# Turning q', k' and the normalised x with VectorE blocks and DMAs in chunks 3 to 5 of a gated linear attention with MLP

## The chip, the cores and the metric

The kernel runs on one core of a Trainium2 chip. Its engines work in parallel, each through its own list of instructions in order: TensorE (PE, with its weight loads as PEld), VectorE (DVE), ScalarE (ACT), GpSimd (POOL) and SyncE (SP), which here issues nearly all transfers; the transfers themselves run on 16 DMA engines. The metric is the device time of one execution in microseconds, lower is better.

## The reference

```python
# gla_recurrent: q, k, v, alpha are (B=4, H=8, S=768, D=48)
for t in range(S):
    state = alpha[:, :, t, :, None] * state + np.einsum('bhd,bhe->bhde', k[:, :, t], v[:, :, t])
    y[:, :, t] = np.einsum('bhd,bhde->bhe', q[:, :, t], state)
# bridge: (B, H, S, D) -> (B, S, H*D = 384)
x = np.ascontiguousarray(y.transpose(0, 2, 1, 3)).reshape(B, S, H * D)
# metaformer_identity: w_ch1 is (384, 1536), w_ch2 is (1536, 384)
mu = np.mean(x, axis=-1, keepdims=True)
var = np.mean((x - mu) ** 2, axis=-1, keepdims=True)
xn = (x - mu) / np.sqrt(var + 1e-06) * g_ln
out = x + np.maximum(xn @ w_ch1, 0.0) @ w_ch2
```

All is float32; the weights come as float64 and are rounded on the chip.

## The kernel before

The sequence is cut into 6 chunks of 128 steps; with 4 batch entries that makes 24 attention turns `attention(c, b)`. In the order they have the letters a to x: chunk c and batch entry b have letter number 4c + b, so m to p are chunk 3, q to t chunk 4 and u to x chunk 5. A "batch" below is one such turn.

One attention turn works as follows. ScalarE takes the logarithm of alpha (`la`, L292); TensorE sums it along the steps with a triangular matrix (`lps`, L303); ScalarE makes of the sum the decay `eq` and its inverse (L306, L307). VectorE makes k' = k times the inverse decay (L309) and q' = q times the decay (L311), side by side in a tile `qk` with the 128 steps on the partitions. The decay at the end of each half chunk goes to DRAM as `row` (L316) and comes back as the column `gate` (L378).

For the scores, q' and k' are needed with the head's 48 elements on the partitions and the steps along the row. TensorE turns them: for each of the two, four transpositions of 128x112 into one PSUM tile `tps` (L336), which ScalarE (in chunk 0 for k' VectorE) copies to the SBUF tiles qT and kT (L343, L341). These are the operands of the scores `aps` (L360). VectorE masks the scores into `at` (L372). TensorE makes the state updates `ups` from k' and v (L388); VectorE and GpSimd put them through the gate into the states (L401, L403). The output `yps` adds scores times v and qT times state (L426, L429).

The output goes to a DRAM tile `kept` (L452, to be read back as `ob` for the residual, L493), is normalised by ScalarE to `xn` (L460 to L470), and TensorE turns it with three transpositions of 128x128 into `xps` (L476). From there VectorE (chunks 0 and 1) or ScalarE (chunks 2 to 5, three instructions, L483) writes it to the chunk's tile xT, multiplied by g_ln. xT holds all four batch entries of a chunk, and the MLP starts when it is complete.

The MLP of chunk 0 is plain: `hps` (L506) and `ops` (L518). Chunks 1 to 5 use a scheme with fewer products of blocks: sums of blocks of xT are made first (`combine_x`, L769, letter X), then 30 hidden products (L795) whose results VectorE and GpSimd add up; ScalarE applies the ReLU (L846, letter R); sums of hidden blocks are made (`combine_hidden`, L605, letter N); 20 projections (L618) are added to `ob`, and finished quarters are sent (`send`, L497).

Who does what when is written out by hand: each letter of the string `ORDER` resumes one of these generators until its next `yield`. M is the MLP of the chunks 1 to 5, V the hidden products of chunk 5, A to L the rounding of the weights, S and W sums of weights, Y, Z, P, Q the MLP of chunk 0, O the loads of `ob`. Since each engine works in order, `ORDER` fixes the list of every engine, the queue of SP among them: a transfer that waits for its data holds up all transfers behind it. All transfers of the kernel but two small ones at the start are issued on SP.

Tiles come from pools with a fixed number of buffers per tag; a new tile waits until the oldest buffer's readers are done. qT and kT share the tag `sum` (11 buffers) with the sums of blocks and the partial results `u`; the input tiles ra, rk, rq have the tag `in` (6 buffers), with two batch entries in each tile. From chunk 3 on `load_one` loads alpha, k and q of one batch, two batches ahead; it is called right after the step at L316.

Of the kernel before, what the change touches and what calls it, by code (L numbers as in the profile page):

```python
# [9 lines left out]
FP32 = mybir.dt.float32  # L10
# [5 lines left out]

EPS = 1e-6
STAGED = 3

# [1 line left out]


ORDER = (
    "acacababcdaacabdbaabdcacabbacbbababceccbaAcfcdbadaacecacfeafdeeeabfddaddbbbceeeA"
    "caecdfeedcgadeehbbbbeegfgbgdhddgaAbaghffffgbdgAgehefhffgecfffBddccicdChjfcYehhhc"
    "fhfcdieYdgggehghejhgjfhffdfYhjjjjidBZYBZeiZijZijAhghgiBghiiijBZCZZkCCYkiZiijlYij"
    "lejjkYhgYkiZDYhZZhkDYYZggYkkkljkhfhgDCkiEilEYlgEFEYDlZZFlZhgliFYFjillYYYYZjHHlmk"
    "lSklkjlGkYkYYGZZZZiZZZlnGiinmZHgmgglllmkmngYIQimYmjmmInjmQjlGikoIkmOIfheHlkkSjjo"  # L30
    "hkghhiSiJnJmmmmmkSPoPknnJoPeLjSPKkQSeeenLjKnnQpOKnepOSnOlonSffpfnLmnWnmmSSPPSfmP"
    "pghPfjhmmgpSXlmjXXkXXkXkinkQSXWXmnSQOXQQlXiMkiiiXWMWnMMMMSlMMMSSMMkpMMMMMMMoMMnr"
    "oMMoMoWpkqpopMMMMOnqopoopoprmRRmpWpopnMpRpmMoqqnMWrqMMqWRRMMMMMMMWMpMMMMMMMOMqqq"
    "lMMpMMjMjMMMqMpMMqnrrsjoRRRrostMtRqoqqqqoppnooWqpqWoNWNMqRRRMMNNqMMNNsMsslONNsNM"
    "MMMMMMMMMMMMNpmmNMWNmMMqllpllooONMoMMMMMpNNttoMMtosumssMMNrMMrrrMMstMMMrXXXXXXXs"
    "vqqqrvrrXXXMMMMMXrrMMMMMMMMMMMMMMnMnRpJnOqopOMMMMMMMMMMMMMMMMMMMMMMMMpMpRMMtMMRM"
    "MOnMRttrnrurMssssttttsrrvvvrsrstttRtRMtMMtMRuuMtMRRNRtMRuNNNMMMMMRNNMNMMMruqNMMM"
    "MMMMooMMMsssNNNqMqNvNvMvwvMxMMMMNMMMMvNNuuuusrsvuwsquuuuvuuuMussxxvsxvvtvtXvXXww"
    "wXXwXXXXMMMMMMMMMMMMMMMMMXXxMMMMMMMMMMMMMMMMMMMMsvvOORtxtstRttOrMMMMMMMMMMMMMMMM"
    "MMMMMMMxRxMMtxxwrwwwrMMMsxMRwxRwxwxxwwvRxxwuwRvqwRRRuuMwMNMMMMrOxRMRMNMstMxMwNNN"  # L40
    "NNMxxxwwwwwxxNMNMuuNxMwwMNuuNMMMMMxMuMMMNMMMMqNrwXNNXvvvXvvMMuMMXXXXXOMMMMMMMMXM"
    "MOMMMMXXMMMMMMMMMMMMMMMMMMMMMMMMMMMMMMMMMMMMMMMMMRMMMMMMMMMMRRRRMMMMMRuRRROOxMMw"
    "RvNMNNNxRNRvNNNNMMMMMMMMMMMMMNNNXXXXXXXXXXXMMMMMMNVVMMMMVVVVVVVVVVVVVVMMNNVVKVVV"
    "VVVVVVVVOVVVVVVVVMMVVVVVVVVVVVVVVVVVVVVNVVVRRRRRRRRRRRRMMMMMNNNNNONLMMMMONMMNNNN"
    "MMMMMMMMMMMNNMOMMMMMMMMMMMMMNNMMMMMMNMMMMMMMMM"
)


# [1 line left out]
def kernel(  # L50
# [60 lines left out]
    HS = P // 2  # L111
    halves = [slice(HS * s, HS * s + HS) for s in range(2)]
    r = np.arange(P)
# [5 lines left out]
    def load_exchanged(t, src):  # L119

        for h in range(2):
            nc.sync.dma_start(t[halves[h]].rearrange("t i p d -> t (i p d)"),
                              src[halves[1 - h]].rearrange("t h d -> t (h d)"))

    def load(c, m, names):

        bs = range(2 * m, 2 * m + 2)
        rows = slice(c * P, (c + 1) * P)
        for n, src in (("a", alpha), ("k", k), ("q", q)):
            if n in names:  # L130
# [9 lines left out]
                raws.update({(n, c, b): t[:, b - bs.start] for b in bs})  # L140
        if "v" in names:
# [19 lines left out]
    def load_one(n):  # L161

        c, b = divmod(n, B)
        for n, src in (("a", alpha), ("k", k), ("q", q)):
            if n not in lone:
                lone[n] = raw.tile([P, 2, 2, NP, D], FP32, name=f"r{n}", tag="in", bufs=6)
            t = raws[n, c, b] = lone[n][:, b % 2]
            rows = src[b, c * P:(c + 1) * P]
            if n == "a" and b % 2:
                load_exchanged(t, rows)  # L170
                continue
            nc.sync.dma_start(t.rearrange("t i p d -> t (i p d)"),
                              rows.rearrange("t h d -> t (h d)"))
# [92 lines left out]
    def qk_of(c, b):  # L266
        return qks[b if c < 2 else b % 3]
# [10 lines left out]
    def attention(c, b):  # L278
# [39 lines left out]
        n = c * B + b + 2  # L318
        if c < 2 and b % 2:
            load(c + 1, b // 2, "akq")  # L320
        elif n == 3 * B + 1:
            load_one(n - 1)
            load_one(n)
        elif 3 * B + 1 < n < NCB * B:
            load_one(n)
        yield
# [4 lines left out]
        kT = work.tile([R, NP, 2, HS], FP32, name="kT", tag="sum", bufs=11)  # L331
        qT = work.tile([R, NP, 2, HS], FP32, name="qT", tag="sum", bufs=11)
        for i in range(2):
            tps = ps.tile([R, NP, P], FP32, name="tps", tag="bank", bufs=8)
            for p in range(NP):
                nc.tensor.transpose(  # L336
                    tps[:, p], qk_of(c, b)[:, i, p].rearrange("p a b -> p (a b)")[:, :R], ident)
            yield
            tv = tps.rearrange("r p (s t) -> r p s t", s=2)
            if i:  # L340
                (nc.vector.tensor_copy if whole else nc.scalar.copy)(out=kT, in_=tv)  # L341
            else:
                nc.scalar.copy(out=qT, in_=tv)  # L343
            yield
# [84 lines left out]
                            nc.tensor.matmul(yps[r][halves[s], i, p], of, by, start=True, stop=True)  # L429
        yield  # L430
        x = work.tile([P, DM], FP32, name="x", tag="row", bufs=8)
        few = work.tile([P, 5], FP32, name="few", tag="few", bufs=8)
        mean, dev, rstd, off, more_of = (few[:, i:i + 1] for i in range(5))
        act = nc.scalar.activation
        yps = [y.rearrange("t a b d -> t (a b d)") for y in yps]
# [35 lines left out]
        yield  # L471
        if c not in xT_of:
            xT_of[c] = work.tile([P, NF, B, P], FP32, name="xT", tag="xT")
        xps = ps.tile([P, NF, P], FP32, name="xps", tag="bank", bufs=8)
        for f in range(NF):
            nc.tensor.transpose(xps[:, f], xn[:, f * P:(f + 1) * P], ident)  # L476
# [112 lines left out]
    def combine_hidden(c):  # L589
        a, ready = blocks_of(c)  # L590
        n0, n2, n6, n9, n5, n13 = (
            work.tile([P, NT, P], FP32, name=f"sum{i}", tag="sum", bufs=11) for i in range(6))
# [17 lines left out]

    def product(c, n):
        if n == SECOND[0]:
            u = [work.tile([P, 512], FP32, name="u", tag="sum", bufs=11) for i in range(3)]
# [135 lines left out]
    def combine_x(c):  # L749
# [3 lines left out]
            buffers_of_last()  # L753
            new = late_of["x"]
        for i in range(0 if new else 5):
            t = work.tile([P, NT, P], FP32, name=f"sum{i}", tag="sum", bufs=11)
# [20 lines left out]
    def hidden_product(c, r, n):  # L777
# [4 lines left out]
        if n == FIRST[0]:  # L782
            for i in range(3):
                u = late_of["u"][i] if c + 1 == NCB else work.tile(
                    [P, 512], FP32, name="u", tag="sum", bufs=11)
# [123 lines left out]
```

## Time and profile before

| | |
|---|---|
| three runs | 431.96, 433.00, 433.22 us; median 433.0 |
| profiled execution | 433.49 us, of which the profile's span covers 431.6 |
| turns of q' and k', L336 | 192, in the span from 10.1 to 286.3 us; chunks 3 to 5 have half of them |
| turns of x, L476 | 72, from 29.3 to 351.5 us; chunks 3 to 5 have half |
| copies of qT and kT by ScalarE | 44 in all, 586 and 593 ns each |
| scaling of xT by ScalarE, L483 | 48, 365 ns each |
| to landing, median | `kept` 2.8 us, `ob` 2.5, `gate` 4.6, v 6.0 |
| SP's longest sums of waits | for results to send (L497) 60.7 us on GpSimd and 41.4 and 33.0 on VectorE; for the decay (L316) 40.4 on ScalarE |

A share of busy time is a mean over the span. TensorE's instructions overlap, so the length of one (274 ns for a transposition) is more than the distance from one to the next; the distance is read from the chain of waits, where a run of equal instructions stands with its count and length. TensorE's granted clock is full throughout.

### The profile page before, as it was taken

Reading aid. Unit: us, or ns where it says so; the run is one execution under the profiler, and the core shown is the slowest. Engines: PE = TensorE matmul, PEld = TensorE weight load, DVE = VectorE, ACT = ScalarE, POOL = GpSimd, SP = SyncE. Lnnn points to the kernel's source line nnn. Section 1 sums busy time; section 2 is a strip of 40 time slices with the busy share of each in tenths; the row PEclk is TensorE's granted clock in tenths of the full one; section 3 lists DMA queues with packets and bytes.
Section 4 is the critical chain, followed back from the end, with each engine's and each line's share of the span. In section 5 each row is a group of like instructions: output and inputs, shape, how many; then the busy total and the mean of one; then the engine's idle time right before and its main releaser. Section 6 shows DMA issues by size and latency. Waiting matters only on the chain.

```text
span 431.6 us, 11685 instructions
## 1 busy us (share of the span) xinstructions
PE 423.8 (98%) x4760; PEld 378.5 (88%) x4760; DVE 333.0 (77%) x644; ACT 202.4 (47%) x519; POOL 153.1 (35%) x164
## 2 busy tenths in 40 slices
PE   7999998999999999999999999999999999999997
PEld 5889887876678989998899999899998899989996
DVE  3897889789989879958569876567686669856972
ACT  5587654567454754462664351654821461125100
POOL 1012020020113665052674223771044660468414
PEclk9999999999999999999999999999999999999999
DMA  8968878498017343343006033300122000101021
GB/s 252 283 181 259 260 218 288 105 292 256 5 58 220 79 128 94 94 148 93 0 4 175 10 79 115 69 3 2 56 75 91 2 1 2 36 2 37 27 65 55
DMA packets 55517, 45.53 MB, mean 106 GB/s; under 512 B 26748, under 2 KB 51580, under 8 KB 55464
## 3 DMA queue, kind: packets, MB, share of 16 engines
q1 hardware_dynamic: 54920, 44.63, 35.5%
q8 instruction: 37, 0.61, 0.6%
q10 hardware_dynamic: 544, 0.17, 0.2%
q14 instruction: 16, 0.13, 0.1%
HBM read 35.25 MB, written 9.53 MB: 104 GB/s over the span
## 4 chain that ended last, share of the span: by engine, by line
PE 96%; DMA 1%; SPq 0%; issue 0%; DVE 0%; ACT 0%; DVEq 0%
PE ops L618 30%; PE hps L795 30%; PE hps L506 7%; PE ops L518 7%; PE tps L336 5%; PE aps L360 4%; PE ups L388 3%; PE yps L426 2%; PE yps L429 2%; PE xps L476 2%; DMA rq<-in_q_dram 1%; PE lps L303 1%; PE aps L352 1%; PE yps L414 1%; SPq L137 0%
## 5 line engine op out<-in xcount | busy, mean ns | idle before, releaser
L634 POOL TENSOR_TENSOR ob<-ob,u 128x192 f32<-128x192 f32 x40 | 28.2, 714 | 82.9 <-DVE ob L631 61.8
L795 PE MATMUL hps<-sum,w 128*128 128x256 f32 x192 | 47.4, 380 | 0.0
L403 POOL TENSOR_TENSOR mid<-mid,gate 112x192 f32<-112x192 f32 x20 | 13.6, 681 | 78.8 <-DVE mid L401 35.7
L618 PE MATMUL ops<-w,hT 128*128 128x192 f32 x224 | 40.2, 327 | 0.0
L795 PEld LDWEIGHTS hps<-sum,w 128*128 128x128 f32 x192 | 35.9, 190 | 4.6
L618 PEld LDWEIGHTS ops<-w,hT 128*128 128x128 f32 x224 | 36.7, 190 | 0.3
L795 PE MATMUL hps<-xT,w 128*128 128x256 f32 x136 | 34.5, 380 | 0.0
L846 ACT ACTIVATE hT<-hT 128x512 f32<-128x512 f32 x48 | 27.6, 628 | 13.6 <-DVE hT L838 4.5
L506 PE MATMUL hps<-xT,w 128*128 128x256 f32 x144 | 33.2, 383 | 0.0
L518 PE MATMUL ops<-w,hT 128*128 128x384 f32 x96 | 32.6, 489 | 0.0
L506 PEld LDWEIGHTS hps<-xT,w 128*128 128x128 f32 x144 | 26.6, 190 | 3.6 <-issue 0.2
L618 PE MATMUL ops<-ws,sum 128*128 128x192 f32 x160 | 28.8, 326 | 0.0
L628 DVE TENSOR_TENSOR ob<-ops,ob 128x192 f32<-128x192 f32 x50 | 17.1, 352 | 14.8 <-PE ops L618 4.5
L795 PEld LDWEIGHTS hps<-xT,w 128*128 128x128 f32 x136 | 25.5, 190 | 3.3
L460 ACT ACTIVATE xn<-x,few 128x384 f32<-128x384 f32 x24 | 14.7, 615 | 27.8 <-DVE few L456 27.4
L518 PEld LDWEIGHTS ops<-w,hT 128*128 128x128 f32 x96 | 17.7, 190 | 10.8
L618 PEld LDWEIGHTS ops<-ws,sum 128*128 128x128 f32 x160 | 26.3, 190 | 0.1
L814 POOL TENSOR_TENSOR hT<-hT,u 128x512 f32<-128x512 f32 x8 | 10.2, 1276 | 41.5 <-DVE u L813 41.5
L336 PE MATMUL tps<-consts,qk 128*112 128x128 f32 x176 | 23.5, 274 | 1.2 <-DVE qk L311 1.2
L336 PEld LDWEIGHTS tps<-consts,qk 128*112 128x112 f32 x176 | 20.0, 134 | 4.1 <-DVE qk L311 1.8
L618 PE MATMUL ops<-ws,hT 128*128 128x192 f32 x128 | 23.4, 326 | 0.0
L343 ACT COPY qT<-tps 112x512 f32<-112x512 f32 x24 | 14.1, 586 | 18.6 <-PE tps L336 18.4
(243 smaller groups left out, 1178.9 us busy)
## 6 DMA issues: line engine op xcount, KB each, us to landing
ws<-in_moe_w_ch_dram SPq DMA_DIRECT2D x12, 768.0 KB
vn<-in_v_dram SPq DMA_DIRECT2D x12, 384.0 KB, 6.0
kept<-x SPq DMA_DIRECT2D x24, 192.0 KB, 2.8
ob<-kept SPq DMA_DIRECT2D x24, 192.0 KB, 2.5
out_dram<-ob SPq DMA_DIRECT2D x19, 192.0 KB, 1.9
ra<-in_alpha_dram SPq DMA_DIRECT2D x14, 192.0 KB, 4.9
rk<-in_k_dram SPq DMA_DIRECT2D x6, 384.0 KB
rq<-in_q_dram SPq DMA_DIRECT2D x6, 384.0 KB, 4.9
```

Source lines behind the costliest of these rows:

```text
L336: nc.tensor.transpose(tps[:, p], qk_of(c, b)[:, i, p].rearrange("p a b -> p (a b)")[:, :R], ident)
L343: nc.scalar.copy(out=qT, in_=tv)
L360: nc.tensor.matmul(aps[0][halves[i if cross else 1 - i], p, s], kT[rs, p, s], qT[rs, p, s], start=True, stop=True)
L403: nc.gpsimd.tensor_mul(new, new, by)
L460: act(out=xn, in_=x, func=AFT.Square, bias=mean, accum_out=dev)
L506: nc.tensor.matmul(hps, w1[:, j // 2, f, j % 2 * P:][:, :P], xT_of[0][:, f, bs], start=(f == 0), stop=(f == NF - 1))
L518: nc.tensor.matmul(ops_of[b], hT_of[c][:, j, b], w2[:, j], start=(j == 0), stop=(j == NJ - 1))
L618: nc.tensor.matmul(acc, lhs[:, j], rhs[:, j], start=(j == 0), stop=(j == NT - 1))
L628: nc.vector.tensor_add(x, acc, x)
L634: getattr(nc.gpsimd, f"tensor_{op}")(x, x, y)
L795: nc.tensor.matmul(acc[:, i], w, b, start=True, stop=True)
L846: nc.scalar.activation(out=x, in_=x, func=AFT.Relu)
```

## The change

For the batches m to x (chunks 3 to 5, `turned`: letter number 12 and up) TensorE's turns are replaced:

- q and k of a batch are loaded into one joined tile `rj`, side by side (`load_joined`), in place of two tiles.
- After q' and k' are made, one VectorE instruction transposes each 32x32 block of the 128x768 elements of both, back into the joined tile.
- `turn_out` moves the blocks to their places: four DMAs write 32 partitions each to a DRAM tile `rows`, in pieces of 32 elements (128 bytes).
- Only then does `load_one` of the batch after next follow, since it writes to the same joined tile.
- Four DMAs read qT and kT from `rows`, in runs of 128 elements (512 bytes). The copies from PSUM are dropped.
- xn is turned in the same way: a VectorE block transposition (128x384) into a new tile `xt`, four DMAs to `xrows`, one DMA back into xT, and three ScalarE multiplications by g_ln in place.

The tag `sum` has 12 buffers in place of 11, the tag `few` 5 in place of 8. `ORDER` is a new string throughout, from the first lines on; it has 1578 letters in place of 1566.

```diff
+TURNED = 12
...
+    def turned(c, b):
+        return c * B + b >= TURNED
+
+    def load_joined(c, b, t):
+
+        for i, (n, src) in enumerate((("q", q), ("k", k))):
+            raws[n, c, b] = t[:, i]
+            nc.sync.dma_start(t[:, i].rearrange("t i p d -> t (i p d)"),
+                              src[b, c * P:(c + 1) * P].rearrange("t h d -> t (h d)"))
+        raws["j", c, b] = t.rearrange("t n i p d -> t (n i p d)")
+
+    def turn_out(rows, t):
+
+        for a in range(4):
+            nc.sync.dma_start(rows.rearrange("(k j) t -> j k t", j=32)[:, :, 32 * a:32 * (a + 1)],
+                              t[32 * a:32 * (a + 1)].rearrange("j (k i) -> j k i", i=32))
...
+        if not turned(c, b):
+            qT, kT = turned_tiles()
+        if turned(c, b):
+            joined = raws.pop(("j", c, b))
+            nc.vector.transpose(
+                out=joined, in_=qk_of(c, b).rearrange("t n p i c -> t i n p c")[:, :, :, :, :D])
+            yield
+            rows = dram.tile([2 * DM, P], FP32, name="rows", tag="rows")
+            turn_out(rows, joined)
+            yield
+            load_next()
+            yield
+            qT, kT = turned_tiles()
+            src = rows.rearrange("(i n p d) t -> i n d p t", i=2, n=2, p=NP)
+            for i, t in enumerate((qT, kT)):
+                for h in range(2):
+                    nc.sync.dma_start(t[64 * h:64 * h + D].rearrange("r p s t -> r p (s t)"),
+                                      src[h, i])
+            yield
+        for i in range(0 if turned(c, b) else 2):
             tps = ps.tile([R, NP, P], FP32, name="tps", tag="bank", bufs=8)
...
-        few = work.tile([P, 5], FP32, name="few", tag="few", bufs=8)
+        few = work.tile([P, 5], FP32, name="few", tag="few", bufs=5)
...
+        if turned(c, b):
+            xt = work.tile([P, DM], FP32, name="xt", tag="row", bufs=8)
+            nc.vector.transpose(out=xt, in_=xn)
+            yield
+            rows = dram.tile([DM, P], FP32, name="xrows", tag="xrows")
+            turn_out(rows, xt)
+            yield
+            nc.sync.dma_start(xT_of[c][:, :, b], rows.rearrange("(f p) t -> p f t", p=P))
+            yield
+            for f in range(NF):
+                nc.scalar.mul(xT_of[c][:, f, b], xT_of[c][:, f, b], g_col[:, f:f + 1])
+            yield
+            return
         xps = ps.tile([P, NF, P], FP32, name="xps", tag="bank", bufs=8)
```

More of the change, by code (lines that the diff above doesn't have):

```diff
@@ L18 @@
 STAGED = 3
+TURNED = 12
 ORDER = (
[L26 to L43, printed above, removed]
@@ L44 @@
-    "VVVVVVVVOVVVVVVVVMMVVVVVVVVVVVVVVVVVVVVNVVVRRRRRRRRRRRRMMMMMNNNNNONLMMMMONMMNNNN"
-    "MMMMMMMMMMMNNMOMMMMMMMMMMMMMNNMMMMMMNMMMMMMMMM"
+    "acacababcdaacabdbaabdcacabbacbbababceccbaAcfcdbadaacecacfeafdbeeddddaabbcaefbeee"
+    "eafgdddafhfccghfbbefdAbbbahAdibefdbjciecejfgdfffAheeYBccffegdChhfcciedggYfdYheeh"
+    "edcicdiBggihehfYegiAgdiBidgehghghghjihhZZgZZBkjigffBfejfghjkhiiilYCiYCgCDCZYZkkZ"
+    "fZeeYgijDgYZehZhDgYYffjjjYZZkkYEYEeFggElhFjjjhihEFFijlliglZfDZZYSZZZZZYZHSfilkij"
+    "gkkjlHklZlZiIjGkSllkSlZikGlIklnYhkhkGgjGOlOYlmIjYYYYYYjmnlljjkIiHSjnekQnPeOkggJm"
@@ new lines @@
+    "hnhmkPJkgmnHkmLkJfKmnLlmfLQQQKKhSnhWWkgkPmShWonQgQXolpOljpQSkkooXolmnpmSnWmnmkXm"
+    "jnlnPmmXSoSipXnopnniOSPmppSnmommWnPPPnXiiiiipkMmSXXWnnMMXWXoXMMMSSMpMOkMWMMlMMmM"
+    "MlMMSMQWOMMkMMqMmMrMMMMRMqooorqpppppopnnlpqqpMpMMMrqOWqppqmMMMMMMMMMMjWMMMMMMoqr"
+    "MRRRMMMMMMoRrMJRMRRspRRRoMrooNMllMMMMMMMNjpWNMjMoNoRlooMNloNsrNNNqqqqqqsqqMqMMMr"
+    "MMNMrjMMrpttrjtWNsMstorrrpqqqrssrNMMMNNnnnMMXMMpptrXNMtMMMNMpMXXXXXMpptXMMsMmmmm"
+    "XMMoMMMMMXXqMMoMMMMMMMMMMMMMMtMMMMMOMnMmMMOMMMMMMMrMMMMMMMMoooMMMMMMtMpvmuRvRRRR"
@@ new lines @@
+    "RRtsrrttsvtMousssqtOtttvsssssOMMMvMvuMMusMRRRRMRomoMMMMuMuvttsMtMstNNNNNNnNNNnNN"
+    "tNNsrmrussMMvMMMMMMMnMMMxuuMMMvMMMMpMNNNrwMMMMsMMqwuuxMvvvuwvuuuuxvvtvXvLvttutXX"
+    "MMtuMMXMMXMMXusvsxXXXwMMxXxsxMMMMrxsvvMMMMMMMvvwvqqqqxMMvOXtMMwMMMMvsMMMMMuMMMMM"
+    "MMMMrMMMMMMMMMMMMMMMMMMMMMwtquRxRRRRRRRRRwwswxwxrwxxwxxxwxwORwwwMMMttMMOMMrNOwRq"
+    "NNNNNNxNNNxvqMNqxxsrMMNxrwwNwwMxrMMMMMMMMMMMMrMwMwMMNMNNMXXxXXXXXXXXOwwMMMMMMMMu"
+    "MMMMMMMMMMMMMMxxxXvMMMMMMMMMMMMMMMMMMMMMMMMMMMMMMMMMMMMMwRRRRMMOuuuuuMMMMMMMMMMM"
@@ L46 @@
+    "vwRRRRRwOxNMRMuMNOuNNRMMNMNMXuNNXXXXRXVXXXNXXVMMMMMMMMMMMMMMMMNNVVVVVVVVVVVVVVVV"
+    "VVVVVVVVVVNMNVVVVVVVVMMMNOVVVVVVVVVVVVVRRRMRRVVVNNMMRMMVVVVRRRVVRRVVORNNMMMMMMMM"
+    "MMMMNNNNNNNNNOMNONMMMMMMMMMMMMMMMMMMMMMMNNNMMMMMMMMKMMMMMM"
 )
@@ L128, in load @@
         rows = slice(c * P, (c + 1) * P)
+        joined = turned(c, bs.start)
         for n, src in (("a", alpha), ("k", k), ("q", q)):
-            if n in names:
+            if n in names and not (joined and n != "a"):
                 t = raw.tile([P, 2, 2, NP, D], FP32, name=f"r{n}", tag="in", bufs=6)
@@ L140, in load @@
                 raws.update({(n, c, b): t[:, b - bs.start] for b in bs})
+        for b in bs if joined and "k" in names else ():
+            load_joined(c, b, raw.tile([P, 2, 2, NP, D], FP32, name="rj", tag="in", bufs=6))
         if "v" in names:
@@ L163, in load_one @@
         c, b = divmod(n, B)
[L164 to L173, printed above, removed]
+        if "a" not in lone:
+            lone["a"] = raw.tile([P, 2, 2, NP, D], FP32, name="ra", tag="in", bufs=6)
+        t = raws["a", c, b] = lone["a"][:, b % 2]
+        rows = alpha[b, c * P:(c + 1) * P]
+        if b % 2:
+            load_exchanged(t, rows)
+        else:
+            nc.sync.dma_start(t.rearrange("t i p d -> t (i p d)"), rows.rearrange("t h d -> t (h d)"))
+        if b % 2 not in lone:
+            lone[b % 2] = raw.tile([P, 2, 2, NP, D], FP32, name="rj", tag="in", bufs=6)
+        load_joined(c, b, lone[b % 2])
     consts = cpool.tile([P, 2 * P + HS], FP32, name="consts")
@@ L317, in attention, with load_next @@
         yield
[L318 to L326, printed above, removed]
+        def load_next():
+            n = c * B + b + 2
+            if c < 2 and b % 2:
+                load(c + 1, b // 2, "akq")
+            elif n == 3 * B + 1:
+                load_one(n - 1)
+                load_one(n)
+            elif 3 * B + 1 < n < NCB * B:
+                load_one(n)
+        if not turned(c, b):
+            load_next()
+            yield
         at = ats[b % len(ats)]
@@ L330, in attention, with turned_tiles @@
                 "k (p s t) -> k p s t", s=2, t=HS)
-        kT = work.tile([R, NP, 2, HS], FP32, name="kT", tag="sum", bufs=11)
-        qT = work.tile([R, NP, 2, HS], FP32, name="qT", tag="sum", bufs=11)
-        for i in range(2):
+        def turned_tiles():
+            return [work.tile([R, NP, 2, HS], FP32, name=n, tag="sum", bufs=12)
+                    for n in ("qT", "kT")]
+        if not turned(c, b):
+            qT, kT = turned_tiles()
[7 more added lines that the diff above has]
+            yield
+            load_next()
+            yield
[7 more added lines that the diff above has]
+        for i in range(0 if turned(c, b) else 2):
             tps = ps.tile([R, NP, P], FP32, name="tps", tag="bank", bufs=8)
@@ L473, in attention @@
             xT_of[c] = work.tile([P, NF, B, P], FP32, name="xT", tag="xT")
+        if turned(c, b):
[9 more added lines that the diff above has]
+                nc.scalar.mul(xT_of[c][:, f, b], xT_of[c][:, f, b], g_col[:, f:f + 1])
+            yield
+            return
         xps = ps.tile([P, NF, P], FP32, name="xps", tag="bank", bufs=8)
@@ L591, in combine_hidden @@
         n0, n2, n6, n9, n5, n13 = (
-            work.tile([P, NT, P], FP32, name=f"sum{i}", tag="sum", bufs=11) for i in range(6))
+            work.tile([P, NT, P], FP32, name=f"sum{i}", tag="sum", bufs=12) for i in range(6))
         add, sub = nc.vector.tensor_add, nc.vector.tensor_sub
@@ L612, in product @@
         if n == SECOND[0]:
-            u = [work.tile([P, 512], FP32, name="u", tag="sum", bufs=11) for i in range(3)]
+            u = [work.tile([P, 512], FP32, name="u", tag="sum", bufs=12) for i in range(3)]
             win["u"] = [u[i // 2][:, i % 2 * HM:][:, :HM] for i in range(5)]
@@ L755, in combine_x @@
         for i in range(0 if new else 5):
-            t = work.tile([P, NT, P], FP32, name=f"sum{i}", tag="sum", bufs=11)
+            t = work.tile([P, NT, P], FP32, name=f"sum{i}", tag="sum", bufs=12)
             t = t.rearrange("p a t -> p (a t)")
@@ L784, in hidden_product @@
                 u = late_of["u"][i] if c + 1 == NCB else work.tile(
-                    [P, 512], FP32, name="u", tag="sum", bufs=11)
+                    [P, 512], FP32, name="u", tag="sum", bufs=12)
                 first_of["u", c, i] = u.rearrange("p (j t) -> p j t", j=2)
```

## The prediction

> **What bounds the kernel now.** I read the page first (busy shares and slices), then the chain of waits in order of time, then the groups by line and shape, last the DMA view in short windows.
>
> ```profile
> PE 423.8 (98%) x4760; PEld 378.5 (88%) x4760; DVE 333.0 (77%) x644; ACT 202.4 (47%) x519; POOL 153.1 (35%) x164
> ...
> PE   7999998999999999999999999999999999999997
> ...
> DVE  3897889789989879958569876567686669856972
> ...
> PEclk9999999999999999999999999999999999999999
> DMA  8968878498017343343006033300122000101021
> ```
> TensorE is at work in every slice at full clock; VectorE is nearly full only up to slice 13, and after a third of the span the DMA engines are mostly idle.
>
> ```profile
> 89.00 0.87 PE tps L336 x8
> 89.88 2.58 PE ops L518 x8
> ...
> 216.30 0.33 PE xps L476 x3
> ...
> 323.95 25.90 PE hps L795 x120
> 349.85 0.33 PE xps L476 x3
> 350.18 1.30 PE ops L618 x8
> ...
> 395.91 32.51 PE ops L618 x200
> 428.52 0.36 DVE ob L628
> ```
> The chain (start us, length us, what) runs along TensorE with hardly a gap, from its first transposition at 10 us to 428 us. So each turn is on the path, at its spacing in the chain and not at its 274 ns of pipelined duration: 0.87/8 = 0.109 us for one of q' and k', 0.33/3 = 0.11 us for one of x. In the same way a pass of a hidden product takes 25.90/120 = 0.216 us, of a projection 32.51/200 = 0.163 us. With these I added up TensorE's work through the list of instructions of both kernels. The old list gives 418.7 us, plus 10.5 us before the first; a step's place in the old list and its start in the trace agree within 4 us. Batches go by their letters in the order: m to p are chunk 3, q to t chunk 4, u to x chunk 5. "Place" below is that running sum in the new list, the time at which TensorE would get there without a stall.
>
> **What is removed.** Twelve turns of q' and k' (8 transpositions each) and twelve of x (3 each): 12 x (8 x 0.109 + 3 x 0.11) = 14.4 us, all on the path. ScalarE loses 24 copies of some 0.59 us (L343, L341), 14 us of an engine that is idle half the time: nothing on the path. The 36 scalings of xT stay, with SBUF in place of PSUM as source; I leave their 0.365 us.
>
> **What is added on VectorE.**
>
> ```profile
> L219 DVE SCALAR_TENSOR_TENSOR w<-ws,w 128x768 f32<-128x768 uint32 x12 | 11.7, 974 | 0.4
> L217 DVE TENSOR_SCALAR w<-ws 128x768 int32<-128x768 int32 x12 | 6.6, 552 | 0.0
> 100.00:140.00 40.00, 40.00 (x375) 28.79 (x374) 38.49 (x73) 20.20 (x57) 5.91 (x6) 1.00 0.39 119
> 140.00:280.00 140.00, 140.00 (x1636) 130.52 (x1635) 108.14 (x214) 68.83 (x180) 67.21 (x68) 1.00 0.31 84
> ```
> The first two lines are groups (busy us, mean ns), the others windows with busy us of PE, PEld, DVE, ACT, POOL. The trace has no block transposition. Passes over 128x768 take 0.55 to 0.97 us; I take 0.97, since the source is strided, and 0.55 for 128x384 (L466: 0.47, L311: 0.61). Bounds: 0.55 and 0.47 below, twice my values above, as for two passes. That is 12 x 1.52 = 18 us (12 to 36). VectorE had 32 us idle in 140 to 280 and hardly any in 100 to 140, where four large turns come. I add the durations behind the VectorE work that is placed ahead of them, and find m and n turned at about 98.6, 2 to 3 us behind their place. Cover for the rest: VectorE's idle time. If it is gone, hidden products find no free PSUM bank.
>
> **What is added on the DMA side.** Per batch 4 + 4 issues for q' and k' and 4 + 1 for x, 13 in place of none: 156 more on SP's queue (259 before), at 0.43 us (median of the stores of `kept`) 5.6 us a batch. Nobody waits for SP as such; what matters is when the data land. A store of `kept` lands 2.8 us after issue, a load of `ob` 2.5 us. Each q'k' turn writes 3072 pieces of 128 B, 192 on each of 16 engines, each x turn 96. No 128 B store is in the trace. Nearest rows, two windows of the DMA view:
>
> ```profile
> DMA packets 1012, 0.02 MB, mean 19 GB/s; under 512 B 1011, under 2 KB 1011, under 8 KB 1011
> ## 3 DMA queue, kind: packets, MB, share of 16 engines
> q1 hardware_dynamic: 1011, 0.00, 47.9%
> ...
> DMA packets 144, 0.10 MB, mean 164 GB/s; under 512 B 16, under 2 KB 144, under 8 KB 144
> ## 3 DMA queue, kind: packets, MB, share of 16 engines
> q1 hardware_dynamic: 144, 0.10, 48.4%
> ```
> From 223.9 to 225.0 only 4-byte packets of the gate run: 0.479 x 16 x 1.1 us / 1011 = 8.3 ns each. From 429.7 to 430.3 a 96 KB store of 128 rows of 768 B: 0.484 x 16 x 0.6 / 144 = 32 ns over all, 35 ns for a long one. The line between them gives 13 ns at 128 B, far nearer to the first row; I take c = 13. Bounds 8 and 35. DMA work per batch is then (192 + 96) x 13 ns = 3.7 us, and the loads back are a quarter as many pieces. With batches about 17 us apart and 31% of the engines taken, this fits.
>
> [...]
>
> **Do the data come in time?** From a large turn to the products that read qT (aps) the new list leaves 17 to 31 us of TensorE work: m, n 96 to 115; o, p 119 to 142; q 145 to 167; r 158 to 175; s, t 177 to 214; u, v 218 to 246; x 256 and w 263 to 280. One chain alone needs 1.0 (turn) + 1.7 (four issues) + 2.4 (landing) + 1.7 + 2.1 = 9 us. Three places are tight.
>
> First pair. SP's queue holds eight outward issues, six input loads (the loads into the joined buffers wait for the outward pieces, and all behind them with them), then eight loads of qT and kT. From 98.6 + 0.9: 384 pieces per engine, 0.384c; + 2.4 landing; + 9 issues, 3.9; + 2.1: 107.9 + 0.384c, against 115.4. c = 13: 112.9, in time; c = 26: 2.5 us late; c = 35: 6 us late.
>
> w. SP waits at the sends of chunk 2 until about 253.4. x's outward pieces go at 258.6; its loads wait for them, and behind those stand t's x turn, w's pieces, s's x turn, and w's loads. x's land at X = 258.9 + 0.192c (not before 260.3, the last issue) + 2.4; four loads, one of `ob` and the first of t's stores bring SP to X + 2.5; from there 0.288c for t's and w's pieces, + 2.4, + 1.7 + 2.1 for w's loads. So w lands at 275.1 for c = 13 (place 280.0), 282.5 for c = 26 and 286.8 for c = 35.
>
> u's x. Turned at 332, its four stores are out by 334.5, landed 337, read back 340, scaled (3 x 0.37) 341; combine_x of chunk 5 asks at 341, the first product of its result stands at 352. Some 5 us to spare.
>
> One moved step costs a little: the load of the input v for batches u and v (L143) now stands behind a send that waits for a projection at 240. It is issued at 242.5 and lands 6.0 us later (its median), 248.5; the update products (L388) stand at 248.1: 0.4 us. The two pool edits (`sum` 11 to 12 buffers, `few` 8 to 5) I put at nothing: at most four of `few` are alive at once in the new list, so ScalarE's later work covers it; were it gone, one more wait of a microsecond.
>
> **Sum.** Profiled execution 433.5 us (span 431.6, 1.9 around it): 433.5 - 14.4 + 0.4 = 419.5. Runs have a median of 433.0, 0.5 lower. For margins of 2.5 us at the first pair that need not hold I round up: 420.
>
> **Rivals.**
> A. Short stores cost two of my packets, c = 26: 2.5 us late at the first pair and 2.5 at w, 424.5. For: no row for 128 B stores. Against: stores of 768 and 1536 B (35 and 65 ns) lie nearly on one line with the 4-byte loads. A VectorE at twice my price (36 us) ends alike: it would be some 5 us further behind in 140 to 230, and w comes 3 us later, about 425.
> B. The other side: the DMA engines' time per piece decides, and a 128 B store costs what a 1536 B packet costs (a 192 KB store in the window 263.5 to 264.4: engines 57.9% busy over 0.9 us, 128 packets, so 65 ns). First pair 107.9 + 25.0 = 132.9, 17 us late; w, by the same steps, 21 us; o, p and r some 12 us together: 419.5 + 50 = 470. It decides from about c = 38, where first pair and w (7 and 8) eat the gain. For: four stores write into the same 512 B rows, which nothing here does now. Against: 4-byte packets take 8 ns.
> C. The queue decides, not the bytes: SP stands at a send or at a landing while a load behind it is due, 12 to 16 us over all three tight places. About 433: no change. For: SP's waits already add up to nearly 300 us, most of them at sends (L497). Against: the new list has input loads, not results, behind nearly all of these waits.
> That the turns stay on TensorE can be excluded: the new program has 132 fewer matmuls.
>
> **Chances.** Forecast 0.52 (own range 417 to 423); A 0.16; C 0.08, half of it within 0.3% (about what a measurement here can tell from no change) and the rest split to both sides; B and lesser lateness past the break-even 0.24, 0.02 of it within 0.3%. Faster 0.52 + 0.16 + 0.02 = 0.70, same 0.06, slower 0.22 + 0.02 = 0.24. The range goes from 417 (no stall, and 2 us of TensorE's old gaps gone) through A and C into the beginning of B, 437; what is left out is B's far end.
>
> **What would show it.** Right: half of the 192 turns of q' and k' and of the 72 of x gone, the chain again along TensorE with aps (L407 of the new kernel) waiting under 1 us in all for DMA; block turns near 1 us; packets of 128 B near 13 ns. Wrong: PEld waiting for a DMA of qT or kT at places 115 or 280 (A, B); DMA share near 9 tenths in 100 to 280 (B); SP in one long wait ahead of a load that TensorE then waits for (C); TensorE waiting for VectorE's sums (the VectorE variant).

## The result, and the profile after

The changed kernel takes 417.4 us (median of 4 runs, 417.42 to 419.17) against 433.0 before: ratio 0.966, 95% interval 0.963 to 0.968. Predicted were 420.0 us, 417 to 437. The profiled execution took 417.43 us, its span 415.5, where before it was 433.5 and 431.6. So 16.1 us are to be explained, and the prediction's sum has 14.0 of them.

The page after, first the busy shares and the slices, then the chain that ended last (its shares of the span by engine and by line):

```profile
PE 410.2 (99%) x4628; PEld 364.5 (88%) x4628; DVE 344.7 (83%) x668; ACT 192.7 (46%) x495; POOL 151.2 (36%) x164
...
PE   7999999999999999999999999999999999999997
...
DVE  4898899999999988997699768779767689786773
...
PEclk9999999999999999999999999999999999999999
DMA  8989987768788865336856775763314120101201
...
PE 97%; DMA 1%; SPq 1%; DVE 0%; issue 0%; DVEq 0%
```

TensorE is still the bound. It has 132 matmuls fewer, its busy time is 13.6 us shorter, and its idle time went from 7.8 to 5.3 us: 13.6 + 2.5 = 16.1. VectorE's busy time grew by 11.7 us. (The turns last 18.2 us together, but instructions that follow one another overlap: the first two turns, of 0.97 us each, take 1.83 us together.) The slices of the DMA row from the 11th on are fuller, but VectorE has 0% of the chain and the DMA engines 1%.

The waits of TensorE (us in total, times, longest). Its list has only these two:

```profile
PE tps L383 <- DVE qk L333: 1.2, 1, 1.2
PE lps L266 <- DVE more L263: 1.1, 1, 1.1
```

Both are in the first 10 us, ahead of any turned batch. Nothing in the list waits for a DMA of qT or kT.

Next the block turns (busy us, mean ns), and a window in which only pieces of 128 B run: 158 to 161 us, most of the stores of one turned batch. The DMA line gives the packets, the queue line packets, MB and the share of 16 engines:

```profile
L365 DVE STREAM_TRANSPOSE rj<-qk 128x768 f32<-128x768 f32 x12 | 11.5, 967 | 0.0
...
L523 DVE STREAM_TRANSPOSE xt<-xn 128x384 f32<-128x384 f32 x12 | 6.7, 567 | 1.0 <-ACT xn L517 1.0
```

```profile
DMA packets 2561, 0.33 MB, mean 110 GB/s; under 512 B 2560, under 2 KB 2560, under 8 KB 2560
## 3 DMA queue, kind: packets, MB, share of 16 engines
q1 hardware_dynamic: 2560, 0.32, 69.4%
```

0.694 x 16 x 3.0 us / 2560 = 13.0 ns for a piece of 128 B. The two windows that the prediction showed of before, now (busy us of PE, PEld, DVE, ACT, POOL, then clock, DMA share, GB/s):

```profile
100.00:140.00 40.00, 40.00 (x490) 28.84 (x491) 38.31 (x69) 15.24 (x45) 10.98 (x10) 1.00 0.83 204
140.00:280.00 140.00, 140.00 (x1717) 129.72 (x1713) 117.57 (x236) 69.56 (x181) 68.46 (x71) 1.00 0.63 144
```

The share of the DMA engines went from 0.39 to 0.83 in the first and from 0.31 to 0.63 in the second. VectorE went from 108.1 to 117.6 us in the second; in the first it was full already (38.5 of 40 us before, 38.3 now). TensorE is busy throughout both.

### The profile page after: what moved, and what is told of

It reads as the page before. It is cut to its first block, busy times and chain, and to the rows that moved or that the text cites. A ratio compares the mean times of both kernels' runs of the same rounds, so it can differ in the third digit from the quotient of the medians.

```text
span 415.5 us, 11641 instructions
## 1 busy us (share of the span) xinstructions
PE 410.2 (99%) x4628; PEld 364.5 (88%) x4628; DVE 344.7 (83%) x668; ACT 192.7 (46%) x495; POOL 151.2 (36%) x164
## 4 chain that ended last, share of the span: by engine, by line
PE 97%; DMA 1%; SPq 1%; DVE 0%; issue 0%; DVEq 0%
PE ops L678 32%; PE hps L855 31%; PE hps L566 8%; PE ops L578 8%; PE aps L407 3%; PE ups L435 3%; PE tps L383 3%; PE yps L476 3%; PE yps L473 3%; PE lps L325 1%; DMA rq<-in_q_dram 1%; PE xps L536 1%; PE aps L399 1%; PE yps L461 1%; SPq L156 1%; DVE qk L333 0%
## 5 line engine op out<-in xcount | busy, mean ns | idle before, releaser
L694 POOL TENSOR_TENSOR ob<-ob,u 128x192 f32<-128x192 f32 x40 | 24.7, 629 | 75.7 <-DVE ob L691 55.1
L450 POOL TENSOR_TENSOR st<-st,gate 112x192 f32<-112x192 f32 x16 | 10.7, 671 | 52.6 <-DVE st L448 52.6
L507 ACT ACTIVATE xn<-x,few 128x384 f32<-128x384 f32 x24 | 14.8, 617 | 21.6 <-DVE few L503 15.6
L678 PE MATMUL ops<-more,sum 128*128 128x192 f32 x120 | 22.0, 326 | 0.0
L678 PEld LDWEIGHTS ops<-ws,hT 128*128 128x128 f32 x128 | 21.2, 190 | 0.1
```

The costliest lines, as they stand in the source:

```text
L450: nc.gpsimd.tensor_mul(new, new, by)
L507: act(out=xn, in_=x, func=AFT.Square, bias=mean, accum_out=dev)
L678: nc.tensor.matmul(acc, lhs[:, j], rhs[:, j], start=(j == 0), stop=(j == NT - 1))
L694: getattr(nc.gpsimd, f"tensor_{op}")(x, x, y)
```

## The experiments

All ratios are to the kernel before on the same chip; the changed kernel's 0.9655 is the mark. The kernel before took 432.5 to 433.0 us (medians) throughout, so differences of half a us are not read. "Lag" below is the start of an instruction of TensorE in the experiment less the start of the same instruction in the changed kernel, followed through both traces. Where TensorE makes its first transposition varies among the traces of this document from 9.2 to 10.2 us, and the changed kernel is at the early end; so some lag is there before the edit can act.

### Turns back on TensorE: is it the turns or the new order?

`x_tensor`: x of chunks 3 to 5 on TensorE again.

```diff
         if turned(c, b):
-            xt = work.tile([P, DM], FP32, name="xt", tag="row", bufs=8)
-            nc.vector.transpose(out=xt, in_=xn)
             yield
-            rows = dram.tile([DM, P], FP32, name="xrows", tag="xrows")
-            turn_out(rows, xt)
             yield
-            nc.sync.dma_start(xT_of[c][:, :, b], rows.rearrange("(f p) t -> p f t", p=P))
+            xps = ps.tile([P, NF, P], FP32, name="xps", tag="bank", bufs=8)
+            for f in range(NF):
+                nc.tensor.transpose(xps[:, f], xn[:, f * P:(f + 1) * P], ident)
+            for f in range(NF):
+                nc.scalar.mul(xT_of[c][:, f, b], xps[:, f], g_col[:, f:f + 1])
             yield
-            for f in range(NF):
-                nc.scalar.mul(xT_of[c][:, f, b], xT_of[c][:, f, b], g_col[:, f:f + 1])
             yield
             return
```

> The changed kernel with its new order, but x of chunks 3 to 5 is turned by TensorE again (12 x 3 transpositions, at the step of the load of xT, scaled by ScalarE out of PSUM); q' and k' stay with VectorE and the DMAs. Theory 1 (the gain is the turns taken off TensorE): 12 x 0.33 = 4.0 us come back, 417.4 + 4.0 = 421.4 us, TensorE's busy time up by about 4 from 410.2. Theory 2 (the gain is the new order, the turns would have fitted beside other work): 417.4, within 1 us.

Measured: 430.2 us (428.4 to 432.4), ratio 0.994 (0.992 to 0.996): 12.8 us back, three times the turns. The profiled execution is the longest of the ten, 432.4 us. Its chain of waits around 345 us (start, length, what), and two windows of the same trace, before and after 352.8 (columns as above):

```profile
342.70 0.34 PE xps L526 x3
343.05 0.02 issue
343.07 0.89 ACT xT L528 x3
343.95 2.60 ACT hT L904 x5
346.55 0.04 issue
346.60 1.65 PE ops L676 x4
```

```profile
346.00:352.80 6.80, 6.20 (x21) 6.11 (x22) 4.82 (x10) 2.98 (x8) 0.00 (x0) 0.51 0.00 1
352.80:359.60 6.80, 6.80 (x42) 6.70 (x41) 6.56 (x15) 1.55 (x4) 0.00 (x0) 1.00 0.01 2
```

ScalarE stood 3.8 us at the scaling of xT (L528), which needs the turn, with the activations of hT (L904) queued behind it; TensorE then waited 2.9 us for those. And for the next 6.8 us its granted clock was 0.51: 21 matmuls in the first window, 42 in the second. So one badly placed step, mine and not the change's, cost some 2.9 + 3.4 us in this execution. The lag itself steps by 0.33 us at each group of 3 turns, which is the prediction's price. Of the 14.9 us of lag at the end, 4.0 are the turns, 6.3 that step, 1.4 a wait at 213 for ScalarE (la, L314), and 1.6 had come by 35 us, ahead of the first of these turns; that leaves 1.6 in small steps.

The half clock was not in every execution. The mean granted clock of the ten goes from 1.000 (428.4 us) to 0.992 (432.4 us), and 0.004 of 430 us is 1.7 us, what 3.4 us at half clock cost.

`x_tensor_late`: the scaling one step later, where the changed kernel has it.

```diff
                 nc.tensor.transpose(xps[:, f], xn[:, f * P:(f + 1) * P], ident)
+            yield
             for f in range(NF):
                 nc.scalar.mul(xT_of[c][:, f, b], xps[:, f], g_col[:, f:f + 1])
             yield
-            yield
```

> As the kernel with x on TensorE, but ScalarE scales xT one step after the turn, at the step in which it scales in the changed kernel. In the first of the two, ScalarE stood 3.8 us at the scaling, waiting for the turn, the activations of hT stood behind it, TensorE waited 2.9 us for them, and the granted clock was 0.5 for 6.8 us after. Theory 1 (beyond the 4.0 us of turns the excess is that wait and its clock): no such wait, clock 1.0, 421.4 to 424, ratio to before 0.975 to 0.980. Theory 2 (the excess belongs to the turns themselves, or to PSUM buffers that they hold): 430, ratio 0.994, as before.

Measured: 424.0 us (423.4 to 424.4), ratio 0.980 (0.978 to 0.981), no such wait, and a mean clock of 1.000 in all executions. The chain at two of its turns:

```profile
286.39 0.33 PE xps L526 x3
...
294.51 0.33 PE xps L526 x3
```

Theory 1, at its upper end. Of the lag of 6.9 us at the end, 4.0 are the turns (12 x 0.33), 1.1 had come by 34 us, long before any of them, and the rest are small steps between.

`qk_tensor`: q' and k' of chunks 3 to 5 on TensorE, at a step chosen for each batch, x by DMA.

```diff
-            joined = raws.pop(("j", c, b))
-            nc.vector.transpose(
-                out=joined, in_=qk_of(c, b).rearrange("t n p i c -> t i n p c")[:, :, :, :, :D])
...
+            raws.pop(("j", c, b))
+            place = {12: 3, 13: 2, 14: 3, 15: 3, 16: 3, 17: 2, 18: 2, 19: 2,
+                                            20: 2, 21: 2, 22: 0, 23: 3}[c * B + b]
+            for step in range(4):
+                if step == place:
+                    qT, kT = turned_tiles()
+                    for i, to in enumerate((qT, kT)):
+                        tps = ps.tile([R, NP, P], FP32, name="tps", tag="bank", bufs=8)
+                        for p in range(NP):
+                            nc.tensor.transpose(
+                                tps[:, p], qk_of(c, b)[:, i, p].rearrange("p a b -> p (a b)")[:, :R],
+                                ident)
+                        nc.scalar.copy(out=to, in_=tps.rearrange("r p (s t) -> r p s t", s=2))
+                if step == 2:
+                    load_next()
+                yield
```

> The changed kernel with its new order, but q' and k' of chunks 3 to 5 are turned by TensorE again (12 x 8 transpositions, copied by ScalarE), and x stays with VectorE and the DMAs; the joined input loads stay. Theory 1 (the turns): 12 x 8 x 0.109 = 10.5 us come back, 427.9 us, TensorE's busy time about 420.7. Theory 2 (the order): 417.4, within 1 us. If both this and the kernel with x on TensorE come out as theory 1 says, the two parts add up without touching one another.

Measured: 436.1 us (433.6 to 438.5), ratio 1.008 (1.005 to 1.011), 18.7 us back where 10.5 were expected. The profiled execution was the shortest of them (433.6); from its chain:

```profile
102.88 1.74 DVE ws L638 x2
104.62 0.49 DVE x L490 x2
105.11 0.14 issue
105.24 0.85 PE xps L536 x6
106.09 2.58 PE ops L578 x8
108.67 0.87 PE tps L373 x8
```

The last line is the price: 8 turns, 0.87 us, the same as before the change. The lag steps by just that at all 12 batches, 10.4 us. What comes on top are three waits: 2.1 us at 105 (the chain runs through VectorE until its x is done), 2.0 at 237 and 1.0 at 276, and half a us at 176. That makes 16 of the 16.2 us of this execution. The others are up to 5 us longer, and their mean granted clock goes with it: 1.000 at 433.6 and 434.0 us, 0.995 to 0.996 at 435.2 to 436.2, 0.992 at 437.7 and 438.5. 0.008 of 432 us is 3.5 us, so most of the difference is the clock; where those stretches lie no trace shows.

`all_tensor`: both edits together, so that only the new order is left of the change.

> The new order alone: both q', k' and x of chunks 3 to 5 on TensorE, nothing turned by VectorE or DMAs. Theory 1 (the turns): 417.4 + 14.4 = 431.9 us, that is 1 us under the kernel before, which the new order won elsewhere (the first transposition 0.9 us earlier and a stall of 1.3 us less at 74). Theory 2 (the order): 417 to 425, most of the gain kept.

Measured: 445.6 us (445.1 to 449.2), ratio 1.031 (1.027 to 1.036). Neither theory: the new order with all turns on TensorE is 13 us slower than the kernel before. Its trace has the waits of both parts, the 2.9 us of ScalarE's scaling among them, with the clock at 0.55 over the 3.4 us from 361.2. Of the 27.5 us by which its span is longer than the changed kernel's, 14.4 are the turns, 8.5 more waits of TensorE (10.8 us in its list against 2.3), and 1.7 the clock; 2.9 are not accounted for. As some of these waits belong to my placing, 13 us is more than the order by itself need cost. The run doesn't price the order alone, but nothing in it shows a gain without the change's turns: the new order was made for a TensorE that need not turn. The turns are the gain, but for some 2 us of TensorE's gaps (below).

### The pieces: what does the DMA side bear?

`pieces2` (64 B), `pieces4` (32 B) and `pieces_long` (256 B) differ in one number, the elements in a piece (`w` in the code, not the batch): 16, 8 and 64, where the changed kernel has 32. The bytes and the number of issues stay.

```diff
-            nc.sync.dma_start(rows.rearrange("(k j) t -> j k t", j=32)[:, :, 32 * a:32 * (a + 1)],
-                              t[32 * a:32 * (a + 1)].rearrange("j (k i) -> j k i", i=32))
+            w = 32 // 2
+            nc.sync.dma_start(
+                rows.rearrange("r t -> (r t)").rearrange("(k j a w) -> a j k w", j=32, a=4, w=w)[a],
+                t[32 * a:32 * (a + 1)].rearrange("j (k w) -> j k w", w=w))
```

> The stores of the turned blocks go out in pieces of 64 B in place of 128 B: twice the pieces, the same bytes and issues. The pieces land in DRAM in another arrangement, so what the loads bring back is q', k' and x with their elements in other places; all work after it is the same in kind and size. Theory 1 (the prediction's sums, the price goes by the piece): a piece of 64 B between 8.3 and 13 ns, some 20 ns for 128 B, first pair at 107.9 + 7.7 = 115.6 and w at about 278: 417.4 to 419. Theory 2 (the DMA engines are already at the limit in 100 to 140, 0.83 busy): 422 or more, as in case A at twice the price.

> The stores of the turned blocks go out in pieces of 32 B: four times the pieces, the same bytes and issues; the pieces land in DRAM in another arrangement, so the elements that the loads bring back stand in other places. Theory 1 (the prediction's formulas as they stand): at 4 x 9 = 36 ns for every 128 B the first pair lands at 107.9 + 13.8 = 121.7 against a place of 115.4 and w about 7 us late: some 430 us, TensorE waiting for DMA at both places. Theory 2 (the places have more room than the sums gave, since the first pair came 4 us early in the changed kernel's trace and w 2.8): the waits add up to 5 to 8 us, 422 to 426. Theory 3 (DMA time is fully covered): 417.4.

> The stores of the turned blocks go out in pieces of 256 B: half the pieces, the same bytes and issues; the pieces land in DRAM in another arrangement, so the elements that the loads bring back stand in other places. With 256 B between 13 ns (128 B) and 27 to 31 ns (512 B), some 19 ns, the engines have some 12 us less to do. Theory 1 (at 128 B the DMA time is covered, nothing waits for it): 417.4 within 1.5 us, ratio 0.962 to 0.969. Theory 2 (it is only partly covered, as the 10.6 us that 64 B pieces cost for 25 us of engine time suggest): 412, ratio 0.953.

Mean time of a piece on its engine by the packets of the traces, and the median of the 48 issues of q'k' stores on SP's queue:

| piece | us, ratio (interval) | ns a piece, all pieces on 16 engines | issue |
|---|---|---|---|
| 256 B | 418.1, 0.967 (0.965 to 0.968) | 21.3, 36.8 us | 0.48 us |
| 128 B, the change | 417.4, 0.966 (0.963 to 0.968) | 13.0, 45.1 us | 0.54 us |
| 64 B | 428.1, 0.989 (0.986 to 0.992) | 10.2, 70.5 us | 0.87 us |
| 32 B | 488.3, 1.128 (1.126 to 1.129) | 10.9, 151.2 us | 1.82 us |

At 256 B, 8.3 us less of the engines bring nothing: theory 1, the DMA time of the change is covered.

At 64 B it is no longer: 10.6 us more, the size that theory 2 expected. Its cause is only half shown. Of the 10.1 us of lag 2.0 had come by 47 us, ahead of all stores of turned data; the rest comes in steps of 0.5 to 2 us at the gate, at v, at kT and behind VectorE. The chain of this kernel runs 66% along TensorE, 11% along SP's queue and 8% along DMAs:

```profile
PE 66%; SPq 11%; DMA 8%; DVE 7%; POOL 3%; issue 3%; ACT 0%; POOLq 0%; DVEq 0%; ACTq 0%
```

The engines' share rose from 0.83 to only 0.85 in 100 to 140 and from 0.63 to 0.73 in 140 to 280. The edit lengthens the engines' time and SP's issues together, and this run doesn't separate the two.

At 32 B all three theories were far too low. The page of that kernel, and its waits:

```profile
PEclk9999999997998899799979966997599999999999
DMA  8999787599799897587977696599753353010201
```

```profile
PE aps L409 <- DMA kT<-rows: 26.5, 8, 12.4
PE lps L327 <- ACT la L316: 14.9, 4, 6.7
```

The longest wait is that for batch w, 12.4 us. The prediction's terms for w add up to 270.0 + (0.192 + 0.288)c, which at c = 4 x 10.9 = 43.6 ns for every 128 B gives 290.9 against a place of 280.0, 10.9 us late. (TensorE was by then 55 us behind, so only the distance between the two can be compared.) The first pair's gives 107.9 + 0.384 x 43.6 = 124.6 against 115.4, 9.2 late. Its data were there at 121.7, and TensorE was 9 us late there, but not for them: the gate came first and hid them. The chain at that place:

```profile
106.74 2.25 SPq L141
108.99 0.04 issue
109.03 2.31 SPq L194
...
112.90 3.70 DMA ra<-in_alpha_dram
...
116.67 0.53 ACT la L316
117.20 0.04 issue
117.25 1.54 PE lps L327 x4
```

The loads of alpha for the gate (ra, and from it la and lps) stand behind the stores of the turned pieces (L141) on SP's queue. The first store of this series took 0.34 us to issue; each of the next seven took 1.8 to 2.4, and so did the load of alpha that follows (L194), which has no short pieces. So, as I read it, these issues were held up by the store ahead of them. The gate is late at 108, ahead of any qT, and that wait is in no term of the prediction.

Much of the rest of the 71 us is the clock: its mean is 0.937 over 486.7 us, so 61 us if the rest ran at half (the two stretches of 17.1 us, from 283.7 and from 334.9, have 0.51), worth 30.7 us of full clock, a part of them spent waiting anyway. Each of its six stretches begins within a wait of TensorE of 3 us or more; but a wait of 3.0 us at 177 had none behind it (clock 1.00).

### VectorE: what do the block turns cost?

`turn_twice` does each turn twice into the same place; `turn_short` does nearly none, so what its loads bring back is not turned, with the same transfers.

```diff
             nc.vector.transpose(
                 out=joined, in_=qk_of(c, b).rearrange("t n p i c -> t i n p c")[:, :, :, :, :D])
+            nc.vector.transpose(
+                out=joined, in_=qk_of(c, b).rearrange("t n p i c -> t i n p c")[:, :, :, :, :D])
...
             nc.vector.transpose(out=xt, in_=xn)
+            nc.vector.transpose(out=xt, in_=xn)
```

```diff
-            nc.vector.transpose(
-                out=joined, in_=qk_of(c, b).rearrange("t n p i c -> t i n p c")[:, :, :, :, :D])
+            nc.vector.transpose(out=joined[:, :32], in_=qk_of(c, b)[:, 1, 3, 1, :32])
...
-            xt = work.tile([P, DM], FP32, name="xt", tag="row", bufs=8)
-            nc.vector.transpose(out=xt, in_=xn)
...
-            turn_out(rows, xt)
+            turn_out(rows, xn)
```

> Every turn on VectorE is done twice into the same place (24 more transpositions, 12 x (0.97 + 0.57) = 18.5 us more of VectorE, 344.7 to 363). Theory 1 (the prediction's variant of case A, VectorE at twice the price is some 5 us behind and TensorE waits for it): 422 to 425. Theory 2 (VectorE's idle time in 140 to 280 covers it, and only the four large turns in 100 to 140 show): 417.4 to 419.

> VectorE does almost nothing of the turns: of each q', k' block turn only a 32-column piece is done (so that the stores still wait for VectorE at the same place), and x is stored as it stands, without a turn; stores and loads are the same in number and size, and the elements that come back are not the turned ones. VectorE is relieved of some 17 us. Theory 1 (the turns of the changed kernel lie in VectorE's idle time, only the doubled ones went over): 417.4 within 1.5 us, ratio 0.962 to 0.969. Theory 2 (VectorE is a second bound along the way, and each us on it costs half a us, as in the doubled kernel, 8.2 us for 15.3): 417.4 - 17 x 0.54 = 408, ratio 0.943.

Measured: 425.7 us with the turns doubled, ratio 0.983 (0.982 to 0.985); 418.2 us with nearly none, ratio 0.967 (0.965 to 0.968), so no gain. The page of the doubled kernel, busy shares and the chain by engine:

```profile
PE 412.8 (97%) x4628; PEld 363.9 (86%) x4628; DVE 360.0 (85%) x692; ACT 192.1 (45%) x495; POOL 150.3 (35%) x164
...
PE 71%; DVE 15%; DMA 4%; POOL 3%; SPq 3%; issue 3%; DVEq 0%; POOLq 0%
```

The chain, which ran 97% along TensorE, now passes to VectorE for 15% of the span, and every wait in TensorE's list is for VectorE. The turns of the change fit into VectorE's idle time as far as can be measured: without them it is busy for 330.9 us, 13.8 less, and nothing is gained. The next 15.3 us cost 8.2. By the rate of the doubled kernel taking the turns away would have brought 7 to 9 us, and it brought none. So the cover ends somewhere between the turns done once and done twice; where, these two runs don't show.

### Going further

`x_chunk2` also sends x of chunk 2 through VectorE and DRAM, `x_chunk12` that and three batches of chunk 1; `scale_act` moves the scaling of xT of chunk 1, four passes of VectorE between 87 and 109 us, to ScalarE.

```diff
-        if turned(c, b):
+        early = c * B + b in (8, 9, 10, 11)
+        if turned(c, b) or early:
             xt = work.tile([P, DM], FP32, name="xt", tag="row", bufs=8)
             nc.vector.transpose(out=xt, in_=xn)
-            yield
+            if not early:
+                yield
             rows = dram.tile([DM, P], FP32, name="xrows", tag="xrows")
             turn_out(rows, xt)
-            yield
+            if not early:
+                yield
```

```diff
-        early = c * B + b in (8, 9, 10, 11)
+        early = c * B + b in (4, 5, 6, 8, 9, 10, 11)
```

```diff
-        if c < 2:
+        if c < 1:
             nc.vector.tensor_mul(xT_of[c][:, :, b], xps,
```

> Also x of chunk 2 (four batches, 12 transpositions) is turned by VectorE and through DRAM, in the step in which TensorE turned it, with the scaling in the step that wrote xT. Theory 1 (each turn taken off TensorE counts as long as the data come in time): 12 x 0.11 = 1.3 us less, 416.1. Theory 2 (there, at 140 to 200, SP's queue and VectorE are full enough that the load comes late or pushes others back): 417.4 or more.

> As the kernel with x of chunk 2, and also three batches of chunk 1 (e, f, g; 9 more transpositions). Theory 1: (12 + 9) x 0.11 = 2.3 us less than 417.4, 415.1. Theory 2 (in 80 to 140 VectorE has 1.5 of 40 us free and the DMA engines are 0.8 to 0.9 busy, so what TensorE saves is lost in waits): 417 to 420.

> The scaling of xT of chunk 1 (four passes of 0.55 us at 85 to 103 us) is done by ScalarE, three passes a batch, as in chunk 2, in place of VectorE. Theory 1 (VectorE stands on the path there, as the doubled turns of m and n, 1.2 us late at 98, suggest, at about half a us per us): 4 x 0.55 x 0.54 = 1.2 us less, 416.2, ratio 0.963. Theory 2 (TensorE does not wait for VectorE in the changed kernel): 417.4, ratio 0.9655; ScalarE in its turn late for the gate of chunk 3: above 418.

Measured: `x_chunk2` 437.1 us, ratio 1.010 (1.009 to 1.011), theory 2, though by far more than it named; `x_chunk12` 458.3 us, 1.060 (1.057 to 1.062), far above what either theory allowed; `scale_act` 417.5 us, 0.965 (0.964 to 0.967), theory 2. From the chain of the first:

```profile
124.50 0.49 DVE xt L524
...
127.44 0.64 SPq L140
...
129.22 2.50 DMA xrows<-xt
...
131.84 2.65 DMA xT<-xrows
...
134.51 0.98 ACT xT L534 x3
...
136.78 12.56 PE hps L858 x48
```

From the turn to xT it is 10 us: turn, issues, landing, load. The step in which ScalarE scales comes sooner than that in an order made for a turn on TensorE, so ScalarE stood 18.1 us at the load, with everything behind it; TensorE lost 8.3 us there and 6.6 at 189, where r's kT came late behind the new stores, and the clock was half for 6.8 and 10.2 us after (its mean in this execution: 0.979). Moving a turn takes 0.11 us off TensorE and needs 10 us of lead; here, without an order made for it, it lost. `scale_act` shows that VectorE isn't on the path there, although it is nearly full (19.0 of 20 us from 80 to 100 in the changed kernel). No version was measurably faster than the changed kernel.

## Why the prediction was right, by its steps

**Removed, 14.4 us: right.** In the undone kernels the same turns come back at 0.87 us for 8 and 0.33 for 3, and TensorE's busy time fell by 13.6. ScalarE lost 9.7 us, not 14, off the path: its 36 scalings take 0.393 us from SBUF, not 0.365; the rest of the difference stays open.

**VectorE, 18 us, covered: right.** 967 and 567 ns measured, 0.97 and 0.55 taken; 18.2 us in all. The variant with twice the price was put at about 425, with TensorE waiting for VectorE's sums; the doubled kernel takes 425.7 and waits for such sums. That the figure agrees so closely is luck: 1.4 of the 8.5 us of its lag had come by 35 us, ahead of any turn, and w, which was to come 3 us later, was not waited for.

**DMA, c = 13 ns: right.** 13.0 by the window above. Rival A's 26, two of these packets for a short store, was an assumption: the trace before has no 128 B store. The stores took 13.0 ns, half of it.

**The places.** By the packets of the trace the first pair was there at 108.7 (predicted 112.9) and w at 274.4 (275.1; the prediction's own terms add up to 276.2). TensorE came to them at 112.6 and 277.2 (115.4 and 280.0). Both margins were there: 3.9 and 2.8 us, where 2.5 and 4.9 were worked out. The order of events was right; the sizes were right in part by luck, as TensorE came 2.8 us early at both, and the first pair, 4.2 us early itself, was in time all the same.

**v's load, 0.4 us late: not so.** It went out at 239.4 in place of 242.5, and the update products waited for nothing. The pool edits, put at nothing, were not tried by themselves; no wait in the trace points to them.

**The sum, 419.5, was 2.1 us too high, and the margin of 0.5 us for tight places was not needed.** The mis-sized term is what the sum took as unchanged, TensorE's gaps: 2.5 us less of idle time. The 0.4 us for v fell out as well, and 13.6 in place of 14.4 us is 0.8 the other way: 2.5 + 0.4 - 0.8 = 2.1. The first transposition came at 9.2 us in place of 10.1, as the load of q landed sooner (5.5 us after issue, 6.4 before), and a stall in the old kernel's list of waits isn't in the new:

```profile
PE aps L360 <- issue: 1.3, 1, 1.3
```

Together that is 2.2 of the 2.5 us. The first part is luck, as kernels that start alike vary by as much (9.2 to 10.2 us); why the stall at 74 us went is not shown beyond the order being another. The range's lower end, 417, named just this case: no stall, and 2 us of the gaps gone.

**A and B: right in kind, too cheap.** 26 ns were put at 424.5 us; 64 B pieces, 20.4 ns for 128 B, take 428.1, though with longer issues on SP as well. B was to decide from 38 ns; it decides sooner, as with 20 ns 10.6 of the 15.6 us are gone. The places priced were those of qT, kT and xT, and at 32 B their formulas came within 2 us of the lateness (w 10.9 for 12.4; the first pair's data 9.2 late by the sum, and 8 to 9 late against TensorE's own pace). Left out were the gate's alpha behind the stores on SP, the issues on SP that took longer with more pieces (median 0.54 us at 128 B, 1.82 at 32 B), and the half clock after many of the waits.

**C: not seen.** SP still waits at sends (53.7 us on GpSimd in place of 60.7), and nobody was late for it.

## What to carry to other kernels

Work that left the full engine counted here at its spacing in the chain (0.87 us for 8 turns, 0.33 for 3), in full, as long as what replaced it stayed in idle time. What decided was the lead of each result over its use (3.9 and 2.8 us to spare at the first pair and w; 8.3 us lost in `x_chunk2`, where a turn needs 10 us to xT): work it out for all that shares the queue, not only for the data that moved.

The cover has an edge. 12 us of VectorE's busy time and 45 us of the DMA engines' were free here, and the next 15 and 25 came with 8 and 11 us (the 11 with longer issues on SP among their causes). So a doubled cost and an omitted one have to be run both before a rate is drawn from either.

An order tuned to one division of the work lost with another here, so undoing a part of a change shows its price only where the trace shows which waits the undoing itself brought.

## What was not expected of the hardware

A short wait of TensorE was at times followed by a stretch at a lower clock, so that it cost more than itself. After 2.9 us in the profiled execution of `x_tensor` its granted clock was 0.51 over the next 6.8 us, in `all_tensor` 0.55 over 3.4 us; after the 2.1 us in that of `qk_tensor` it stayed at 1.0. Two stretches in `x_chunk2` are 6.8 and 10.2 us long, two in `pieces4` 17.1: these lengths are near 1, 2, 3 and 5 times 3.4. It doesn't follow every time: a wait of 3.0 us in `pieces4` (at 177 us) had a clock of 1.00 behind it, and the same `x_tensor` ran with a mean of 0.992 in one execution and 1.000 in another. What decides it these traces don't show.

Below 128 B a piece hardly got cheaper: 64 B took 10.2 ns and 32 B 10.9 on its engine, little less than the 13.0 of 128 B, so there the time went by pieces and no longer by bytes. And an issue on SP wasn't constant: the stores of q' and k' take 0.48 us (median) at 384 pieces, 0.54 at 768, 0.87 at 1536, 1.82 at 3072. The price fell on what came behind: with 3072 pieces some stores that were the first of their series still took 0.31 us, while the load of alpha behind a series took up to 2.8.

PE's busy time wasn't a count of work here. With the same 4628 matmuls it was 410.2 us in the changed kernel and 415.3 with pieces of 64 B at a clock of 1.0. The matmuls being the same, the 5 us more may be short waits that count as busy; that is my guess, as the traces don't show them.
